# Pooled attention and a softplus FFN on one core: one transpose for a chunk's last keys, and new priorities for the first part

## The chip, the core and the metric

The kernel runs on one core of a Trainium2 chip. The metric is the device time in microseconds (us) of one execution; three executions of the kernel before took 883.39 to 884.7 us, with a median of 884.19. Five engines matter: TensorE (PE) for matrix products and transposes, VectorE (DVE), ScalarE (ACT), GpSimd (POOL, almost unused here) and SyncE (SP), which issues all the DMAs of the kernel in its own order.

## What is computed

Eight batches, eight heads, 576 tokens, 64 values per head. Keys and values are pooled by means over 8 tokens, so 72 of each remain per head. The attention output of all heads, 512 values per token and 4608 tokens, goes through a feed-forward network of width 2048 with a softplus between.

```python
k_p = k.reshape(B, H, Sp, pool, D).mean(axis=3)          # Sp = 72, pool = 8
v_p = v.reshape(B, H, Sp, pool, D).mean(axis=3)
scores = scale * np.matmul(q, k_p.transpose(0, 1, 3, 2))
scores = scores - np.max(scores, axis=-1, keepdims=True)
attn = np.exp(scores)
attn = attn / (np.sum(attn, axis=-1, keepdims=True) + 1e-09)
x = np.matmul(attn, v_p)              # -> (4608, 512): heads side by side
h = x @ w_in                          # w_in 512 x 2048
g = np.maximum(h, 0.0) + np.log1p(np.exp(-np.abs(h)))
out = g @ w_out                       # w_out 2048 x 512
```

All inputs are float32. For the large products each operand is split into a rounded high part and the rest (the low part), and three products stand for one.

## The kernel before

Tokens are taken in chunks of 256, two tiles of 128 each; there are 18 chunks. A chunk goes through attention (transposes of queries, scores, exponentials, normalisation, transposes of the probabilities, products with the values) and then through the FFN in 16 blocks of 128 hidden values.

The program has two parts, each planned by itself. The first, which ends near 182 us, loads and pools the first batches, converts the weights (seven DVE and ACT steps per block, in `weights`), runs attention for chunks 0 to 3 and the FFN for chunks 0 to 2. The second part runs the rest at a steady pace.

The order inside a part is made by a planner in the kernel's Python code, the class `Order`. Each operation has an engine, a cost in us, the operations it comes after, slots (buffers and PSUM banks that it takes and frees) and a lag. The planner goes forward in its own time: it finds the operation that could end first, and among those that the same engine could start about then it takes the one with the highest `rank + first`. `rank` is the length of the longest chain behind the operation; `first` is a correction. A table named `HASTE` adds such corrections by the operation's number:

```python
for i, x in HASTE.items():
    todo.ops[i + 2].first += x
```

So HASTE and the costs set the order of the first part on PE, ACT, DVE and SP, and which slot each operation gets; they add no instruction. For SP the costs are those of issuing, and the lag of 2.2 or 2.4 us stands for the time until the data has landed. An engine runs its instructions in the planned order and waits on the chip until the real inputs are there.

A query tile of `attend(c)`, chunk c, has 72 probabilities per head: 64 "main" ones and 8 "last" ones. `main` (L447) multiplies the 64 by the reciprocal sum into `pm`, `PT` (L468) transposes them and `PT_out` (L475) copies them. For the last 8 the kernel before does this, tile by tile: `ends` (L454, two DVE instructions) writes the products into `pe` three times side by side, 96 columns for each half of the heads; `last` (L480, two matmuls) transposes them into 96 rows of a PSUM bank; `last_high` (L487, one ACT cast) rounds all 96 rows into the tile `lt_`; `last_low` (L492, one DVE subtraction) turns the middle 32 rows into the low part. `av_products` (L594, L601) needs `pT` and `lt_` of both tiles.

The second part already does it by chunk: `pair_ends` (L563), `pair_last` (L568), `pair_high` (L574) and `pair_low_ends` (L578), for both tiles together.

Exponentials of chunks 0 to 2 are single ACT instructions per head with a running sum (`exp_sum`, L432); those of chunk 3 are one instruction. Exponentials and softplus (L632) use different ACT tables, and every softplus of the first part waits for all exponentials of chunks 0 to 2 (`*exps` in `feed`). The first load of softplus' table is recorded at L632.

Other lines: L347 warm-up products, L358 loads of queries, L387 and L394 transposes and copies of queries, L407 scores, L414 row minima, L906 and L909 loads of weights, L938 to L969 their conversion, L1002 and L1013 loads of keys and values, L1026 the products of the left-over tokens, L1060 and L1067 pooling of keys, L1084 pooling of values, L611 the low part of x, L627 and L652 the two FFN products of the first part, L638 the low part of g.

Of the kernel before, what the change touches and what calls it, by code (L numbers as in the profile page):

```python
# [9 lines left out]
F32 = mybir.dt.float32  # L10
# [98 lines left out]
def pooled_attention_softplus_ffn(  # L109
# [269 lines left out]
    class Tile:  # L379
# [47 lines left out]
        def exp_sum(self, j, ps, tag):  # L427
            if j == 0:
                self.sm = small.tile([P, H], F32, tag="sm" + tag, name="sm")
# [20 lines left out]
        def ends(self):  # L450
            self.pe = one.tile([P, 2, 3, R], F32, tag="pe", name="pe")
            for a in range(2):
                hs = slice(4 * a, 4 * a + 4)
                nc.vector.tensor_tensor(  # L454
                    out=self.pe[:, a].rearrange("p n (h j) -> p n h j", h=4),
                    in0=e_[self.c][:, self.t, hs, KM:SP].unsqueeze(1).to_broadcast([P, 3, 4, KL]),
                    in1=self.sm[:, hs].unsqueeze(1).unsqueeze(3).to_broadcast([P, 3, 4, KL]),
                    op=ALU.mult)

        def norm(self):  # L460
            self.reciprocal()
            self.main()
            self.ends()

# [12 lines left out]

        def last(self, ps):
            for a in range(2):
                nc.tensor.transpose(out=ps[0:3 * R, a * P:(a + 1) * P],  # L480
                                    in_=self.pe[:, a].rearrange("p n k -> p (n k)"), identity=ident)

        def last_high(self, ps):

            if self.c not in last_:
                last_[self.c] = one.tile([3 * R, 2, CT], F32R, tag="Y", name="lt_")
            nc.scalar.copy(out=last_[self.c][:, :, self.ts],  # L487
                           in_=ps[0:3 * R, 0:2 * P].rearrange("p (a i) -> p a i", a=2))

        def last_low(self, ps):  # L490
            o = last_[self.c][R:2 * R, :, self.ts]
            nc.vector.tensor_tensor(  # L492
                out=o, in0=ps[R:2 * R, 0:2 * P].rearrange("p (a i) -> p a i", a=2),
                in1=o.bitcast(F32), op=ALU.subtract)
# [384 lines left out]
    def act(n):  # L879
        return 0.14 + 0.00094 * n  # L880
# [10 lines left out]
    def weights(f):  # L891
# [5 lines left out]
        def load(i):  # L897
            def fn():
                if early:
                    if not i:  # L900
                        x["raw"] = stage_at(f % NS)
# [11 lines left out]
            return op(SYNC, 1.5, fn, slots=[stages[0 if early else i]], lag=2.2)  # L913
# [74 lines left out]
        op(SYNC, 0.9, lambda: nc.sync.dma_start(  # L988
# [585 lines left out]
```

## Time and profile before

| what | value |
|---|---|
| runs, median (lowest to highest) | 884.19 us (883.39 to 884.7) |
| the profiled execution | 883.75 us, span 882.0 us |
| PE busy, share of the span | 867.7 us, 98% |
| DVE, ACT busy | 645.4 us (73%), 418.3 us (47%) |
| mean granted clock of PE | 0.998 |
| DMA | 191.17 MB, mean 217 GB/s |

The span goes from the first to the last instruction; the profiled execution took 1.75 us more. An engine is busy while one of its instructions runs. "Idle" is told with the thing that ended it, which is inferred from semaphores. Where a name is followed by `x2`, two instructions are merged into one row.

### The profile page before, as it was taken

How to read it: one execution, taken by the hardware profiler on the slowest of the kernel's cores; microseconds unless marked ns; L12 is line 12 of the kernel's file. 1: busy time of each engine (PE TensorE's matmuls, PEld its weight loads, DVE VectorE, ACT ScalarE, POOL GpSimd, SP SyncE). 2: the span in 40 equal slices, each digit the busy share in tenths (PEclk: the TensorE clock that was granted, in tenths of full speed). 3: DMA queues.
4: the chain of work that ended last, by engine and by line, in shares of the span. 5: the costliest groups of instructions: out<-in, count | busy, mean ns of one | idle time of the engine just before them, and what ended most of it. 6: DMA issues, size and time to landing. Idle time of an engine off the chain costs nothing.

```text
span 882.0 us, 21268 instructions
## 1 busy us (share of the span) xinstructions
PE 867.7 (98%) x8664; PEld 843.3 (96%) x8664; DVE 645.4 (73%) x1601; ACT 418.3 (47%) x852; POOL 3.8 (0%) x33
## 2 busy tenths in 40 slices
PE   6999999999999999999999999999999999999997
PEld 3699999999999999999999999999999999999997
DVE  5899999888966868687767766778566565747454
ACT  5964443445454544544444445353545354444432
POOL 1000000000000000000000000000000000000000
PEclk9999999999999999999999999999999999999999
DMA  9975545545888668578757775778566566646472
GB/s 270 286 233 184 196 150 169 173 161 174 290 268 268 219 216 283 196 267 249 244 191 256 241 240 192 229 240 260 192 201 228 181 214 207 215 165 224 166 249 82
DMA packets 107089, 191.17 MB, mean 217 GB/s; under 512 B 46064, under 2 KB 60400, under 8 KB 106992
## 3 DMA queue, kind: packets, MB, share of 16 engines
q1 hardware_dynamic: 106992, 189.82, 64.4%
q8 instruction: 68, 1.11, 0.5%
q14 instruction: 29, 0.24, 0.1%
HBM read 167.25 MB, written 22.54 MB: 215 GB/s over the span
## 4 chain that ended last, share of the span: by engine, by line
PE 92%; DVE 3%; SPq 2%; DMA 2%; ACT 1%; issue 0%; DVEq 0%; ACTq 0%
PE h L680 38%; PE m L832 30%; PE acc L652 6%; PE h L627 6%; PE acc L723 3%; PE avp L594 2%; PE sc L515 1%; PE ptp L468 1%; PE qTp L387 1%; PE avp L601 1%; DMA stage<-in_moe_w_out_dram 1%; DMA kvl<-in_v_dram 1%; SPq L358 1%; DMA lst<-in_v_dram 1%; SPq L1013 0%
## 5 line engine op out<-in xcount | busy, mean ns | idle before, releaser
L680 PE MATMUL h<-x,l 128*128 128x256 f32 x2748 | 335.0, 278 | 0.0
L680 PEld LDWEIGHTS h<-x,l 128*128 128x128 f32 x2748 | 321.0, 188 | 1.0
L688 ACT ACTIVATE g<-h 128x512 f32<-128x512 f32 x120 | 71.9, 599 | 263.6 <-PE h L680 263.4
L832 PE MATMUL m<-w,so 128*128 128x256 f32 x1134 | 147.1, 276 | 0.0
L832 PEld LDWEIGHTS m<-w,so 128*128 128x128 f32 x1134 | 137.1, 188 | 0.1
L742 DVE TENSOR_TENSOR sf<-g 128x128 f32<-128x128 f32 x112 | 32.7, 292 | 134.2 <-ACT g L688 134.2
L756 ACT CAST so<-sf 128x512 fp32r<-128x512 f32 x112 | 69.7, 622 | 69.1 <-DVE sf L745 68.3
L832 PE MATMUL m<-w,gh 128*128 128x256 f32 x476 | 91.2, 280 | 0.0
L761 DVE TENSOR_TENSOR so<-sf,so 128x512 fp32r<-128x512 f32 x112 | 77.3, 690 | 18.2 <-ACT so L756 16.5
L832 PEld LDWEIGHTS m<-w,gh 128*128 128x128 f32 x476 | 71.7, 188 | 0.0
L709 DVE TENSOR_TENSOR gl<-g,gh 128x384 fp32r<-128x384 f32 (+1 forms) x120 | 67.4, 561 | 2.8 <-ACT gh L702 2.8
L832 PE MATMUL m<-w,gl 128*128 128x256 f32 x238 | 65.8, 277 | 0.0
L702 ACT ACTIVATE gh<-h 128x384 fp32r<-128x384 f32 (+1 forms) x120 | 59.1, 493 | 0.0
L632 ACT ACTIVATE g<-h 128x256 fp32r<-128x256 f32 x96 | 32.0, 382 | 54.3 <-PE h L627 32.4
L627 PE MATMUL h<-x,w 128*128 128x256 f32 x396 | 49.8, 278 | 0.2 <-ACT g L632 0.2
L627 PEld LDWEIGHTS h<-x,w 128*128 128x128 f32 x396 | 47.1, 188 | 0.6 <-ACT g L632 0.4
L652 PE MATMUL acc<-w,g 128*128 128x256 f32 x264 | 47.0, 279 | 0.0
L832 PEld LDWEIGHTS m<-w,gl 128*128 128x128 f32 x238 | 44.7, 188 | 0.0
L853 DVE TENSOR_TENSOR o<-o,m 128x256 f32<-128x256 f32 x98 | 39.8, 419 | 3.3 <-ACT o L845 0.4
L652 PEld LDWEIGHTS acc<-w,g 128*128 128x128 f32 x264 | 39.8, 188 | 0.1
L652 PE MATMUL acc<-w,gl 128*128 128x256 f32 x132 | 36.6, 277 | 0.5 <-DVE gl L638 0.5
L832 PE MATMUL m<-l,gh 128*128 128x256 f32 x196 | 37.0, 277 | 0.0
(210 smaller groups left out, 1318.2 us busy)
## 6 DMA issues: line engine op xcount, KB each, us to landing
l<-wi SPq DMA_DIRECT2D x224, 512.0 KB
out_dram<-o SPq DMA_DIRECT2D x36, 256.0 KB
q<-in_q_dram SPq DMA_DIRECT2D x32, 256.0 KB
kst<-in_k_dram SPq DMA_DIRECT2D x24, 288.0 KB
vst<-in_v_dram SPq DMA_DIRECT2D x24, 256.0 KB
stage<-in_moe_w_in_dram SPq DMA_DIRECT2D x22, 256.0 KB
stage<-in_moe_w_out_dram SPq DMA_DIRECT2D x11, 512.0 KB
wi<-w SPq DMA_DIRECT2D x11, 512.0 KB
```

The lines of the kernel that those rows point to most:

```text
L627: nc.tensor.matmul(out=ps[:, 0:CT], lhsT=row(w, kc), rhs=x[:, kc], start=first and kc == j == 0, stop=last and kc == KC - 1 and j == 2)
L632: nc.scalar.activation(out=g, in_=ps[:, 0:CT], func=AF.Softplus)
L652: nc.tensor.matmul(out=accs[c][t][:, ns], lhsT=a[:, ts], rhs=w[:, ns], start=f == 0 and n == j == 0, stop=f == FC - 1 and n == 1 and j == ...
L680: nc.tensor.matmul(out=ps[:, k * CT:(k + 1) * CT], lhsT=row(w, kc), rhs=x_[c][i][:, kc], start=first and n == 0, stop=last and n == len(or ...
L688: nc.scalar.activation(out=g, in_=x.rearrange("p (b i) -> p b i", i=P), func=AF.Softplus)
L702: nc.scalar.activation(out=gh, in_=quarters(c, x.rearrange("p (b i) -> p b i", i=P)), func=AF.Softplus)
L709: nc.vector.tensor_tensor(out=gl, in0=quarters(c, g), in1=gh.bitcast(F32), op=ALU.subtract)
L742: tt(out=sf[:, 2], in0=g[:, 0], in1=g[:, 2], op=ALU.add)
L756: nc.scalar.copy(out=so[:, 0], in_=ss[c, u])
L761: nc.vector.tensor_tensor(out=so[:, 1], in0=sf, in1=so[:, 0].bitcast(F32), op=ALU.subtract)
L832: nc.tensor.matmul(out=ms[c][n], lhsT=x, rhs=y, start=u == 0 and j == 0 and n in (1, 6, 5, 4), stop=u == FP - 1 and j == 2 and n in (2, 7, ...
L853: nc.vector.tensor_tensor(out=o, in0=in0, in1=m[n], op=how)
```

## The change

- In the first part too, the last keys are now handled by chunk, with the functions of the second part. `ends`, `norm`, `last`, `last_high` and `last_low` are removed. Per tile there is one `pair_ends` instruction; per chunk there are one pair of transposes, four casts of 32 rows and two subtractions.
- The slot `pe` belongs to a chunk, not to a tile.
- The order in which parts of a thing are first touched is free: `exp_sum` makes its sum tile at the first call, whichever half of the heads it is, and a weight block takes its staging tile at the first of its two loads.
- Costs in the planner are set anew (loads of weights 1.5 to 1.65, of keys and values 1.5 to 1.85, of queries 1.4 to 1.0, stores of converted weights 0.9 to 1.3, FFN products 1.4 to 1.37, the first products on PE higher).
- HASTE is replaced by a table with many more entries. As the change is described, the order of the first 31 loads was held while it was made.
- A way to take all exponentials of a chunk at once is added and switched off (`AT_ONCE = ()`).

```diff
@@ class Tile
         def exp_sum(self, j, ps, tag):
-            if j == 0:
+            if not hasattr(self, "sm"):
                 self.sm = small.tile([P, H], F32, tag="sm" + tag, name="sm")
...
-        def ends(self):
-            self.pe = one.tile([P, 2, 3, R], F32, tag="pe", name="pe")
...
-        def norm(self):
-            self.reciprocal()
-            self.main()
-            self.ends()
...
-        def last(self, ps):
...
-        def last_high(self, ps):
...
-        def last_low(self, ps):
...
@@ weights(f)
-                    if not i:
+                    if "raw" not in x:
...
-            return op(SYNC, 1.5, fn, slots=[stages[0 if early else i]], lag=2.2)
+            return op(SYNC, 1.65, fn, slots=[stages[0 if early else i]], lag=2.2)
...
-        op(SYNC, 0.9, lambda: nc.sync.dma_start(
+        op(SYNC, 1.3, lambda: nc.sync.dma_start(
@@ batch(b)
-        o_left = op(SYNC, 1.3, load_left, slots=[ld], lag=2.2)
-        o_k = [op(SYNC, 1.5, load(k, i), slots=[st[i]], lag=2.2) for i in range(2)]
-        o_v = [op(SYNC, 1.5, load(v, i), slots=[vt[i] or vt[0]], lag=2.2) for i in range(2)]
+        o_left = op(SYNC, 1.35, load_left, slots=[ld], lag=2.2)
+        o_k = [op(SYNC, 1.85, load(k, i), slots=[st[i]], lag=2.2) for i in range(2)]
+        o_v = [op(SYNC, 1.85, load(v, i), slots=[vt[i] or vt[0]], lag=2.2) for i in range(2)]
...
-        o = op(PE, 1.0, left_products, [o_left], [ld, s_left])
+        o = op(PE, 1.0 if b else 1.4, left_products, [o_left], [ld, s_left])
...
-            halves.append(op(PE, 0.1 + 0.28 * N, products, [o, *halves], [st[i], s_k]))
+            halves.append(op(PE, 0.1 + 0.28 * N + (0.4 if b == 0 and i else 0), products, ...
...
-        o = op(PE, 0.45, lambda: k_transposes(bank(s_t, "kT"), x["kp"]), [o, o_kl], [s_kp, s_t])
+        o = op(PE, 0.45 if b else 0.7, lambda: k_transposes(bank(s_t, "kT"), x["kp"]), [o, o_kl],
+               [s_kp, s_t])
@@ attend(c)
-            o_q.append(op(SYNC, 1.4, load,
+            o_q.append(op(SYNC, 1.0, load,
...
-        norms = []
+        norms, s_pe = [], Slot("pe")
...
-            o = op(PE, 0.5, lambda x=x, s=s_q: x.qT(bank(s, "qTp")),
+            o = op(PE, 0.5 if c else (1.1, 0.75)[t], lambda x=x, s=s_q: x.qT(bank(s, "qTp")),
...
-            o = op(DVE, 1.45, x.norm, ends, [*s_E, s_sm, s_pm, s_pe])
+
+            def norm(x=x):
+                x.reciprocal()
+                x.main()
+                pair_ends(c, x, "")
+            o = op(DVE, 1.27, norm, ends, [*s_E, s_sm, s_pm, s_pe])
             e_c.append(o)
-            s, r = Slot("bank"), Slot("bank")
+            s = Slot("bank")
             p = op(PE, 0.5, lambda x=x, s=s: x.PT(bank(s, "ptp")), [o], [s, s_pm])
             lows.append(op(ACT, act(512), lambda x=x, s=s: x.PT_out(s.tile), [p], [s, s_pT]))
-            p = op(PE, 0.3, lambda x=x, r=r: x.last(bank(r, "ltp")), [o], [r, s_pe])
-            h = op(ACT, act(256), lambda x=x, r=r: x.last_high(r.tile), [p], [r, s_lt])
-            lows.append(op(DVE, dve2(256), lambda x=x, r=r: x.last_low(r.tile), [h], [r, s_lt]))
+        s_l = Slot("bank")
+        p = op(PE, 0.25, lambda: pair_last(c, bank(s_l, "ltp")), e_c, [s_l, s_pe])
+        for a in range(2):
+            h = op(ACT, act(256), lambda a=a: pair_high(c, a, s_l.tile, a), [p], [s_l, s_lt])
+            lows.append(op(DVE, dve2(256), lambda a=a: pair_low_ends(c, a, s_l.tile), [h], [s_l, s_lt]))
+        for a in range(2):
+            lows.append(op(ACT, act(256), lambda a=a: pair_high(c, a, s_l.tile, 2), [p], [s_l, s_lt]))
@@ feed(c)
-            before1 = op(PE, 1.4, lambda f=f, s=s: ffn1_products(c, f, bank(s, "h")),
+            before1 = op(PE, 1.37, lambda f=f, s=s: ffn1_products(c, f, bank(s, "h")),
...
-                before2 = op(PE, 1.4, second, [before2, d], [gh, gl, *acc_slots[c]],
+                before2 = op(PE, 1.37, second, [before2, d], [gh, gl, *acc_slots[c]],
...
-    HASTE = {27: -130, 29: -3, 34: -120, 36: -120, 45: 40, 46: 20, 48: -180, 55: -2, 56: -10,
...
+    HASTE = {-2: -1844, -1: 13.6, 0: 1314.2, 1: 1554.7, 2: 1533.4, 3: 346.4, 4: 83.2, 5: 55.3, 6:
...
```

The functions that the first part now calls stood in the kernel already, for the second part:

```python
def pair_ends(c, x, tag):
    if c not in pe_:
        pe_[c] = one.tile([P, T, H, KL], F32, tag="pe", name="pe")
    nc.vector.tensor_tensor(out=pe_[c][:, x.t], in0=e_[c][:, x.t, :, KM:SP],
                            in1=x.sm.unsqueeze(2).to_broadcast([P, H, KL]), op=ALU.mult)

def pair_last(c, ps):
    for t in range(T):
        nc.tensor.transpose(out=ps[0:2 * R, t * P:(t + 1) * P],
                            in_=pe_[c][:, t].rearrange("p h k -> p (h k)"), identity=ident)

def pair_high(c, a, ps, row):
    if c not in last_:
        last_[c] = one.tile([3 * R, 2, CT], F32R, tag="Y", name="lt_")
    nc.scalar.copy(out=last_[c][row * R:(row + 1) * R, a], in_=ps[a * R:(a + 1) * R, 0:CT])

def pair_low_ends(c, a, ps):
    rows, to = (slice(i * R, (i + 1) * R) for i in (a, 1 - a))
    nc.vector.tensor_tensor(out=last_[c][to, a], in0=ps[rows, 0:CT],
                            in1=last_[c][rows, a].bitcast(F32), op=ALU.subtract)
```

More of the change, by code (lines that the diff above doesn't have):

```diff
@@ L476, in PT_out @@
                            in_=ps.rearrange("p (m i) -> p m i", m=HP))
-        def last(self, ps):
-            for a in range(2):
-                nc.tensor.transpose(out=ps[0:3 * R, a * P:(a + 1) * P],
-                                    in_=self.pe[:, a].rearrange("p n k -> p (n k)"), identity=ident)
-        def last_high(self, ps):
[L485 to L488, printed above, removed]
-        def last_low(self, ps):
[L491 to L494, printed above, removed]
     order_dep = mybir.DependencyInfo(mybir.DependencyClass.Sync, mybir.DependencyReason.DATA)
@@ L1068, in products @@
                                      rhs=x["k", i][:, :, r], start=r == 0, stop=r == N - 1)
-            halves.append(op(PE, 0.1 + 0.28 * N, products, [o, *halves], [st[i], s_k]))
+            halves.append(op(PE, 0.1 + 0.28 * N + (0.4 if b == 0 and i else 0), products, [o, *halves], [st[i], s_k]))
         o = op(ACT, act(512), lambda: nc.scalar.copy(
@@ L1094, in pooled_attention_softplus_ffn @@
     qT_done, score_done, av_done, k_ready, v_ready, made = {}, {}, {}, {}, {}, {}
+    AT_ONCE = ()
     def attend(c):
@@ L1130, in attend @@
                        [s, s_mn])
-                if c < N1:
+                if c < N1 and c not in AT_ONCE:
                     def exp_sum(x=x, i=i, s=s, e=s_E[0], t=t, n=s_sm):
-                        if c == 0 and 0 not in e_:
+                        if 0 not in e_:
                             new_E(0)
@@ L1140, in less @@
                     def less(x=x, i=i, s=s):
-                        if c not in e_:
+                        if c in AT_ONCE:
+                            if 0 not in e_:
+                                new_E(0)
+                            e_[c] = e_[0]
+                        elif c not in e_:
                             new_E(c)
                         x.less(i, s.tile)
-                    ends.append(op(DVE, 0.46, less, [d, *e_free], [s, s_mn]))
-            if c < N1:
+                    ends.append(op(DVE, 0.46, less, [d, *(e_free if c == N1 else ())], [s, s_mn, *s_E]))
+            if c in AT_ONCE:
+                o = op(ACT, 0.68, lambda x=x: exponential(e_[c][:, x.t]), ends, s_E, table="exp")
+                exps.append(o)
+                ends = [op(DVE, 0.76, lambda x=x, n=s_sm: x.sum(n.name), [o], [s_sm, *s_E])]
+            elif c < N1:
                 exps.extend(ends)
```

13 lines of the change are left out of this document (3 added, 10 removed), and 92 rows, old and new, of the table HASTE.

## The prediction

> **What bounds the kernel now.** I read the page first, then a table of stages, then TensorE's waits in the early stage, and last the rows of the instructions that the change touches.
>
> ```profile
> span 882.0 us, 21268 instructions
> PE 867.7 (98%) x8664; PEld 843.3 (96%) x8664; DVE 645.4 (73%) x1601; ACT 418.3 (47%) x852; POOL 3.8 (0%) x33
> ```
>
> TensorE (PE) is busy 867.7 of 882.0 us, so no order of the work can take out more than 14.3 us, and less work on PE shortens the kernel only where PE is full. The table of stages says where that is (columns: the stretch and its length, then busy time and instructions of PE, PE weight loads, DVE, ACT and POOL, granted clock, DMA share, GB/s):
>
> ```profile
> 0.00:20.00 20.00, 13.23 (x106) 6.95 (x106) 12.05 (x22) 10.17 (x41) 2.36 (x19) 0.91 0.91 261
> 20.00:46.00 26.00, 23.36 (x308) 17.62 (x307) 21.24 (x51) 23.76 (x93) 0.00 (x0) 1.00 0.96 299
> 46.00:182.00 136.00, 135.69 (x1264) 133.74 (x1264) 126.35 (x228) 59.39 (x135) 0.00 (x0) 1.00 0.54 177
> 182.00:870.00 688.00, 688.00 (x6932) 677.89 (x6931) 480.39 (x1290) 322.95 (x582) 1.46 (x14) 1.00 0.66 223
> 870.00:882.00 12.00, 7.40 (x64) 7.10 (x62) 5.36 (x14) 1.98 (x4) 0.00 (x0) 1.00 0.11 44
> ```
>
> The first part of the program ends near 182 us. PE stands idle 6.77 us before 20, 2.64 from 20 to 46, 0.31 from there to 182, never from 182 to 870, and 4.60 in the drain at the end, which the change does not touch. So whatever the first part saves on PE moves the end by as much, and all that a new order can save lies before 46 us. The waits of PE in 0 to 45 us (who waited, for whom, total, times, longest):
>
> ```profile
> PE qTp L387 <- DVE stage L943: 2.3, 1, 2.3
> PE warm L347 <- DVE ones L342: 1.5, 1, 1.5
> PE kps L1067 <- DVE kvst L1060: 1.1, 1, 1.1
> PE kvlp L1026 <- DMA kvl<-in_v_dram: 1.0, 1, 1.0
> PE kps L1067 <- DMA kvst<-in_k_dram: 0.8, 1, 0.8
> PE ltp L480 <- DVE pe L454: 0.8, 2, 0.5
> PE avp L594 <- DVE lt__503 L492: 0.4, 1, 0.4
> PE sc L407 <- ACT qT L394: 0.3, 1, 0.3
> PE ptp L468 <- DVE x L611: 0.2, 1, 0.2
> PE sc L407 <- ACT kT L265: 0.2, 1, 0.2
> ```
>
> The first five rows, 6.7 us, are the start of the program and arriving data. The 2.3 us are put down to a DVE instruction that has nothing to do with queries; a transpose of queries waits for its load, so I read that row as a DMA. The last five, 1.9 us, are matters of order between engines. Two of them, 1.2 us together, hang on the very tiles that the change reworks, pe and lt.
>
> The early stage has a second loss, the clock:
>
> ```profile
> 12.20:15.80 3.60, 0.63 (x4) 0.95 1.11 295
> 15.80:19.20 3.40, 3.36 (x9) 0.55 0.98 274
> L1067 PE MATMUL kps<-kvst,zm x20: 379/390/660, 6.0 to 27.6; 128*64 128x256 f32 x20
> ```
>
> Behind 3.6 us in which PE (first figure after the length) worked 0.63, the granted clock fell to 0.55 for the next 3.4 us; the key products there took up to 660 ns where the shortest took 379. At full clock this stretch is worth about 3.4 x (1 - 0.55) = 1.5 us less.
>
> **The change part by part.**
>
> *Transposes on PE.* Each tile now has a transpose of its pe, as a pair of matmuls; afterwards each chunk of two tiles has one pair. Eight pairs become four. What a pair costs is read from its start to the next start, once in the loose early stage and once in the dense one:
>
> ```profile
> 25.22 0.42 PE L480 MATMUL ltp<-ident,pe 128*96 128x128 f32 x2
> 25.48 0.60 PE L468 MATMUL ptp<-ident,pm 128*128 128x128 f32 x4
> 71.07 0.38 PE L480 MATMUL ltp<-ident,pe 128*96 128x128 f32 x2
> 71.21 0.96 PE L627 MATMUL h<-x,w 128*128 128x256 f32 x6
> ```
>
> 0.26 us early, 0.14 late. Three pairs go from the stretch before 50 us and one from the dense stretch: 3 x 0.26 + 0.14 = 0.92 us at most, and 0.14 at least, if the early ones only lengthen waits. I take -0.5.
>
> *The products pe on DVE.* Per tile two instructions of 96 columns become one of 64:
>
> ```profile
> L563 DVE TENSOR_TENSOR pe<-E,sm x28: 216/219/223, 212.8 to 816.6; 128x64 f32<-128x64 f32 x28
> L454 DVE TENSOR_TENSOR pe<-E,sm x16: 250/252/254, 18.7 to 68.2; 128x96 f32<-128x96 f32 x16
> ```
>
> The new form is already run in the second part of the program (first row). 8 x (2 x 0.252 - 0.219) = 2.3 us of DVE time go. DVE is 82% busy in 20 to 46 and 93% after, and PE hardly waits for it after 46, so I price this at nothing by itself; it shortens the two waits of PE on pe and lt, which are in the holes below.
>
> *The casts on ACT.* This is the part that costs. Per chunk two casts of 96 rows become four of 32 rows, and rows cost no time:
>
> ```profile
> L487 ACT CAST lt__372<-ltp x2: 369/370/371, 22.6 to 25.7; 96x256 fp32r<-96x256 f32 x2
> 218.93 0.74 ACT L574 CAST lt__3134<-ltp 32x256 fp32r<-32x256 f32 x2 [0.77 <-PE ltp L568]
> 219.70 0.41 DVE L578 TENSOR_TENSOR lt__3134<-ltp,lt__3134 32x256 fp32r<-32x256 f32 x1 [1.33 <-ACT lt__3134 L574]
> 220.15 0.36 ACT L574 CAST lt__3134<-ltp 32x256 fp32r<-32x256 f32 x1 [0.48 <-DVE lt__3134 L578]
> 220.54 0.41 DVE L578 TENSOR_TENSOR lt__3134<-ltp,lt__3134 32x256 fp32r<-32x256 f32 x1 [0.42 <-ACT lt__3134 L574]
> 220.99 0.36 ACT L574 CAST lt__3134<-ltp 32x256 fp32r<-32x256 f32 x1 [0.48 <-DVE lt__3134 L578]
> 41.95 1.28 ACT L632 ACT_TABLE_LOAD   x1
> ```
>
> Eight more casts of 0.36 us, 2.9 us in all, six of them for the three early chunks: 2.2 us. And the second part shows how they run: cast, low part and cast on one tile wait for each other in turn, 218.93 to 221.35, 2.4 us, and ACT, which works in order, stood 0.48 us twice. Behind such a cast wait the exponentials of the next tile, and behind the last exponential the table load at 41.95 and every softplus; PE waits for that. From 20 to 46 ACT is busy 23.76 of 26 us, so 2.24 us of slack. Lower end 0 (the casts fill ACT's gaps, or stand behind the table load), upper end 2.2 + 3 x 2 x 0.48 = 5.1 less 2.24 of slack = +2.9. I take +0.5, nearer the lower end, since only the casts of two chunks need come before the table load.
>
> *Slot of pe.* It is held for a chunk now, not a tile, so the next chunk's products wait for this chunk's one transpose. The two norms of a chunk follow each other on DVE anyway: nothing, up to 0.3 where a transpose is late.
>
> *Priorities and the planner's costs.* No instruction and no DMA is added or dropped by them; they set the order of PE, ACT, DVE and SP up to 182 us. With the order of the first loads held, the five waits for start and data (6.7 us) mostly stay. In reach are the 2.64 us of 20 to 46 and 0.31 behind, 2.95 in all: from 0 to -2.95, and below that a loss if new waits come up. I take -1.8: the 1.2 us on pe and lt have half their instructions gone, and a third of the other 1.75. For the start I take -0.4 of the 6.7 + 1.5 us. This end is open on both sides: SP has one wait that an order could shorten,
>
> ```profile
> SPq L358 <- PE qTp L387: 4.5, 2, 2.7
> ```
>
> a load of queries held up to 2.7 us until a transpose on PE had read the buffer. If that transpose goes sooner, the load does; if it goes later, every load queued on SP behind it is late too.
>
> *Second part.* Its plan begins from the first one's ends, but PE is busy 688.00 of 688.00 us there: nothing.
>
> *Sum.* -0.5 + 0.5 - 1.8 - 0.4 = -2.2 us. The profiled execution took 883.75 us, 1.75 more than its span, which gives 881.55. The median of the runs, 884.19, lies 0.44 above that execution, so the time I predict on the runs' scale is 884.19 - 2.2 = **882.0 us**. A measurement of this kernel can tell about 0.2%, 1.77 us, from no change: faster means below 882.4, slower above 886.0.
>
> **The rivals.**
>
> *The holes at the start close too* (chance 0.16). The 2.7 us wait of SP speaks for it: transposes of the first queries put ahead of other early PE work let the load go sooner. Then about half of the 2.3 us hole goes, 1.0, and the slow clock behind it, 1.45: -2.2 - 2.45 = -4.65, 879.5 us. Against it: held loads, with a DMA share of 0.91 already before 20.
>
> *The holes move, they do not close* (0.22): the priorities do not do what they are set for. The planner counts 2.2 us from issue to landing, whatever the load of the DMA engines, which are 0.96 busy from 20 to 46; an order that is tight by its own costs meets late data elsewhere. Then -0.5 and +0.5 stay and a quarter of the holes, -0.7: 883.5 us.
>
> *The clock* (0.08): PE is thinned out again ahead of a dense stretch and a second stretch of 3.4 us runs at 0.55: +1.5 on the forecast, -0.7, 883.5 us. The Trainium skill, in "TensorE: Matmul & The Clock Gate", Part 1: The HAM clock gate, says that the slow clock is the default, that about one window of 3.4 us without enough work brings it back, and that the windows run freely; the trace agrees with that (0.63 us of work in 3.6, then 0.55). By the rule the loss comes or goes whole, with the place of the work in the window; my sum holds a mean between.
>
> *ACT becomes the early bound* (0.20, slower). Place: ACT from 20 us to the table load. Price: all six casts and their six stalls ahead of it, 5.1 - 2.24 = +2.9 us, less 0.5 on PE: +2.4, 886.6 us. It decides from the point where casts and stalls together exceed 2.24 us. For it speaks the serial chain at 218.93; against it that the casts can wait behind the table load, as the row of 41.95 allows for the third chunk.
>
> **How the numbers follow.** The forecast has 0.34, with its own range of 880.7 to 882.4. Faster: 0.34 + 0.16 = 0.50. Within 0.2%: 0.22 + 0.08 = 0.30. Slower: 0.20. The range of 879.0 to 886.2 reaches from below the first rival to half of the last one.
>
> **What would show it.** After the change ltp must be eight matmuls with 64 columns up to 100 us, and pe eight instructions near 0.22 us. PE's idle time from 20 to 182 should fall from 2.95 to about 1.2, the first table load should stand near 41 us, and the span should be near 880. Right steps with a wrong total would show in PE's busy time: more than 1 us less of it would mean that the clock or the transposes were undersized. I am wrong if the table load comes later than 43 us, if ACT waits for low parts before it, if SP issues one of the early loads later than now, or if PE has new waits between 46 and 150, where DVE has little to spare.

## The result, and the profile after

The kernel after takes 889.5 us (median of 6 runs, 886.42 to 890.55), the kernel before beside it 884.39 us (6 runs, 882.84 to 884.92). The ratio is 1.0057 with a 95% interval of 1.004 to 1.0074: slower by about 5 us, where 2.2 us less had been forecast. Three executions of the kernels below, of 969 to 2233 us, were disturbed and stand in no median here.

The profiled execution took 889.96 us. Its page begins so:

```profile
span 888.2 us, 21256 instructions
PE 870.5 (98%) x8656; PEld 846.0 (95%) x8656; DVE 645.0 (73%) x1593; ACT 420.5 (47%) x860; POOL 3.8 (0%) x33
```

The span is 6.2 us longer than the 882.0 of before. PE has 8 matmuls less, and is busy 2.8 us *more*; it also stands idle 3.4 us more. Both need an explanation. The table of stages, with the columns of the prediction's table:

```profile
0.00:20.00 20.00, 14.24 (x138) 7.54 (x138) 10.73 (x17) 8.72 (x30) 2.37 (x19) 1.00 0.88 255
20.00:46.00 26.00, 20.41 (x264) 14.90 (x254) 20.48 (x42) 21.19 (x91) 0.00 (x0) 0.98 0.96 295
46.00:182.00 136.00, 134.32 (x1208) 132.94 (x1209) 120.57 (x218) 59.73 (x143) 0.00 (x0) 0.99 0.50 164
182.00:870.00 688.00, 688.00 (x6946) 677.38 (x6945) 484.86 (x1298) 326.65 (x593) 1.47 (x14) 1.00 0.67 225
```

From 182 us on nothing has changed: PE is full. Idle time of PE is 5.76 us up to 20 (before 6.77), 5.59 from 20 to 46 (before 2.64) and 1.68 from 46 to 182 (before 0.31). The holes of 20 to 182, which the new order was to close, went from 2.95 to 7.27 us.

**Where the new idle time comes from.** PE's waits up to 46 us (who waited, for whom, total, times, longest):

```profile
PE avp L568 <- ACT lt__586 L541: 2.1, 1, 2.1
PE kps L1034 <- DVE kvst L1027: 1.6, 2, 1.1
...
PE avp L568 <- ACT lt__407 L541: 1.0, 1, 1.0
...
PE ltp L535 <- DVE pe L530: 0.3, 1, 0.3
```

Two of them, 3.1 us, hang on the casts into `lt_` (L541; names of lines are those of the kernel after). All engines' waits from 20 to 62 us name the chain behind them:

```profile
DVE stage L905 <- DMA stage<-in_moe_w_out_dram: 3.6, 2, 2.4
ACT lt__586 L541 <- DVE lt__586 L545: 2.9, 1, 2.9
...
ACT lt__407 L541 <- DVE lt__407 L545: 1.8, 1, 1.8
```

And the timeline shows it in order of time (start, length, instruction, and in brackets how long its engine was idle before and what ended that):

```profile
33.70 0.47 SPq L873 DMA_DIRECT2D stage<-in_moe_w_out_dram  x1
...
41.80 0.69 DVE L905 TENSOR_SCALAR stage<-stage 128x1024 int32<-128x1024 int32 x1 [2.44 <-DMA stage<-in_moe_w_out_dram]
42.52 0.69 DVE L910 TENSOR_SCALAR stage<-stage 128x1024 f32<-128x1024 f32 x1
43.23 0.84 DVE L545 TENSOR_TENSOR lt__586<-ltp,lt__586 32x256 fp32r<-32x256 f32 x2
...
44.11 0.36 ACT L541 CAST lt__586<-ltp 32x256 fp32r<-32x256 f32 x1 [2.87 <-DVE lt__586 L545]
...
44.52 0.98 PE L568 MATMUL avp<-lt__586,vlo 96*128 96x256 f32 x4 [2.13 <-ACT lt__586 L541]
...
48.47 1.28 ACT L599 ACT_TABLE_LOAD   x1
```

A weight load issued at 33.70 has landed only by 41.8, 8.1 us later. DVE stands still for it with the first step of the weight's conversion. Behind that step in DVE's order are two low parts of chunk 1's last keys. Behind these the fourth cast waits on ACT: it writes other rows of `lt_` than the low parts and only reads, as the second of them does too, the same 32 rows of the transposes; it waits for them all the same. PE's products with the values wait for the cast, and behind the cast on ACT come exponentials, so the table load comes at 48.47, not 41.95. The same chain had run once before, for chunk 0, from 30.78 to 32.36 us. In the kernel before, the low parts of chunk 0 stood ahead of that conversion (rows of the kernel before, same view):

```profile
26.16 0.42 DVE L492 TENSOR_TENSOR lt__372<-ltp,lt__372 32x256 fp32r<-32x256 f32 x1
...
30.35 0.74 PE L601 MATMUL avp<-lt__372,vlo 96*128 96x256 f32 x4
30.89 0.69 DVE L938 TENSOR_SCALAR stage<-stage 128x1024 int32<-128x1024 int32 x1 [0.77 <-DMA stage<-in_moe_w_out_dram]
```

The load itself is nearly as late in the kernel before: that of the same block was issued at 33.19 us and landed at 39.16. There DVE comes to this block's first step only at 47.5 us, long after the low parts of chunk 1.

How much hangs on this chain differs between executions. after_flip (see The pace) has the same order up to 70 us; there the load had landed by 39.5 us, and PE waited 0.7 us for the casts in place of 3.1. Its idle time from 20 to 182 us was 6.36 us all the same. Two other waits stand in the profiled execution of every kernel with the new order, and not in those of before and before_again (rows of after_flip, then of order_alone, which has the old form of the last keys):

```profile
PE ptp L456 <- DVE pm L449: 1.7, 1, 1.7
...
PE sc L409 <- ACT qT L396: 1.3, 2, 1.0
...
PE avp L571 <- ACT lt__586 L544: 0.4, 1, 0.4
```

```profile
PE ptp L463 <- DVE pm L447: 2.4, 2, 1.9
```

In the first, the transposes of chunk 2's second tile stand in PE's order ahead of FFN products, while ACT still computes that tile's exponentials (1.3 us near 50 us in after, 1.7 to 1.9 in the six others). In the second, scores near 21 us wait 0.97 us for the copy of their queries, in before 0.29. Neither hangs on the casts.

**Where the longer busy time comes from.** The table of stages over a stretch in which PE is full in both kernels and runs almost only the FFN's 256-column products, first before, then after:

```profile
100.00:150.00 50.00, 50.00 (x444) 50.00 (x443) 47.46 (x86) 20.17 (x49) 0.00 (x0) 1.00 0.51 173
```

```profile
100.00:150.00 50.00, 50.00 (x427) 50.00 (x426) 43.91 (x73) 18.79 (x46) 0.00 (x0) 1.00 0.39 131
```

In the same 50 us at the same granted clock of 1.00, PE did 444 products before and 427 after: 112.6 against 117.1 ns each. The groups of the first FFN product from 60 to 170 us (count: shortest/median/longest ns) tell the two apart too, before and after:

```profile
L627 PE MATMUL h<-x,w x335: 276/276/386, 59.8 to 148.7; 128*128 128x256 f32 x168
```

```profile
L594 PE MATMUL h<-x,w x348: 276/281/385, 61.9 to 147.7; 128*128 128x256 f32 x174
```

So the same product has two paces: a recorded length of 276 ns goes with 113.3 ns from start to start (mean of the gaps between neighbours from 100 to 150 us), 281 ns with 117.8. A pace holds for a whole dense stretch and changes at the small groups between (four transposes, scores). After the change one unbroken stretch of 744 products, 82.7 to 170.3 us, ran at the slow pace: 744 x 4.5 ns = 3.3 us. The kernel before had a shorter slow stretch, 1.5 us, between 185 and 250 us, which the kernel after has not (0.4).

The sum for the two profiled spans, in us: idle time from 20 to 182 +4.3, and pace up to 250 us +2.1 (the gaps between neighbouring products above 113.3 ns, added up: 4.4 against 2.25). In the opening the clock became full only at about 10.7 us, where before it was full from 5.2 on (rows below); half of PE's busy time until then makes +2.1, and PE, working slower, waited 1.0 less for the loads. Each has one more stretch at half the clock, of 3.4 us, and the difference there is 0.2. That makes +7.7; the spans differ by 6.2, so some 1.5 us of PE's work are gone. The opening's share is chance: before_again, the same program as before, was at full clock only from 10.6 us on. Without it (+2.1 and -1.0) the difference is 5.1 us, about that of the medians.

### The profile page after: what moved, and what is told of

The parts are those of the page before. It is cut to its first block, busy times and chain, and to the rows that moved or that the text cites. A ratio compares the mean times of both kernels' runs of the same rounds, so it can differ in the third digit from the quotient of the medians.

```text
span 888.2 us, 21256 instructions
## 1 busy us (share of the span) xinstructions
PE 870.5 (98%) x8656; PEld 846.0 (95%) x8656; DVE 645.0 (73%) x1593; ACT 420.5 (47%) x860; POOL 3.8 (0%) x33
## 4 chain that ended last, share of the span: by engine, by line
PE 94%; DMA 3%; DVE 2%; SPq 1%; ACT 0%; issue 0%; DVEq 0%; ACTq 0%
PE h L647 37%; PE m L799 30%; PE acc L619 7%; PE h L594 7%; PE acc L690 2%; PE avp L561 2%; PE qTp L387 2%; PE ptp L453 2%; PE sc L482 1%; PE avp L568 1%; DMA kvst<-in_k_dram 1%; DMA stage<-in_moe_w_out_dram 1%; DMA vst<-in_v_dram 1%; PE kps L1034 1%; PE ltp L535 0%; PE m L482 0%
## 5 line engine op out<-in xcount | busy, mean ns | idle before, releaser
L594 PE MATMUL h<-x,w 128*128 128x256 f32 x396 | 52.0, 286 | 0.3 <-DVE x L578 0.2
L594 PEld LDWEIGHTS h<-x,w 128*128 128x128 f32 x396 | 49.2, 193 | 0.9 <-DVE x L578 0.4
```

Of the source, the lines that this page charges most:

```text
L594: nc.tensor.matmul(out=ps[:, 0:CT], lhsT=row(w, kc), rhs=x[:, kc], start=first and kc == j == 0, stop=last and kc == KC - 1 and j == 2)
```

## The experiments

Each is compared with the kernel before in runs beside it. The table collects them: ratio of times with its interval; PE's idle time up to 20 us and from 20 to 870 us; the loss to the clock (half of PE's busy time while the granted clock was half, or ahead of the first record of the clock); the loss to the pace up to 250 us, as above; what is then left over of the span's difference from before, which is work added or taken out and the error of this reckoning; the recorded length of the FFN's products in 60 to 170 us; the profiled span. All but the ratio and ns in us. One profiled execution stands for each kernel, while the times spread over some 3 to 6 us.

| kernel | ratio (95%) | idle to 20 | idle 20 to 870 | clock | pace | left over | ns | span |
|---|---|---|---|---|---|---|---|---|
| before | 1 | 6.77 | 2.95 | 3.2 | 2.2 | 0 | 276 | 882.0 |
| after | 1.0057 (1.004 to 1.0074) | 5.76 | 7.27 | 5.5 | 4.4 | -1.5 | 281 | 888.2 |
| pair_alone | 1.0077 (1.0047 to 1.0106) | 5.95 | 3.65 | 7.8 | 5.9 | -1.0 | 281 | 889.3 |
| order_alone | 1.0088 (1.0065 to 1.0112) | 5.43 | 8.52 | 6.6 | 2.6 | 0.4 | 276 | 890.4 |
| casts_first | 1.004 (1.0025 to 1.0056) | 4.04 | 6.51 | 6.5 | 1.3 | -1.4 | 276 | 883.9 |
| lows_first | 1.0055 (1.0032 to 1.0078) | 6.13 | 7.61 | 3.3 | 1.0 | -1.0 | 276 | 883.9 |
| both | 1.007 (1.0049 to 1.009) | 3.97 | 7.53 | 6.7 | 1.4 | -1.2 | 276 | 885.2 |
| before_again | 0.999 (0.9975 to 1.0006) | 6.41 | 2.45 | 5.5 | 0.7 | -0.4 | 276 | 881.5 |
| before_flip | 1.0035 (1.0016 to 1.0055) | 6.29 | 2.40 | 7.6 | 4.5 | 0.4 | 281 | 888.0 |
| after_flip | 1.0052 (1.0034 to 1.0071) | 5.76 | 6.36 | 5.6 | 4.3 | -0.6 | 281 | 888.4 |
| pair_012 | 0.9997 (0.9984 to 1.001) | 5.84 | 2.60 | 8.5 | 1.2 | -1.8 | 276 | 883.3 |
| before_warm | 0.9987 (0.9975 to 1.0) | 4.65 | 2.18 | 3.9 | 0.6 | 2.5 | 276 | 880.7 |
| after_warm | 1.0068 (1.0055 to 1.0081) | 3.89 | 6.62 | 4.3 | 4.5 | 0.9 | 281 | 887.2 |
| pair_012_warm | 1.0008 (0.9997 to 1.002) | 5.18 | 2.85 | 1.9 | 1.4 | 2.4 | 276 | 880.7 |

The seven kernels with the new order are idle 6.4 to 8.5 us from 20 us on, the seven with that of before 2.2 to 3.7. That part of the loss belongs to the order. Clock and pace fall differently within either group.

### Half of the change at a time

*The pairing in the order of before* (pair_alone): costs, HASTE and order of before, the last keys by chunk, their four casts and two low parts at the second tile's places.

```diff
             self.main()
-            self.ends()
+            pair_ends(self.c, self, "")
...
+            def high(x=x, r=r):
+                if x.t == 1:
+                    for a in range(2):
+                        pair_high(c, a, r.tile, a)
+                    for a in range(2):
+                        pair_high(c, a, r.tile, 2)
```

> The kernel before with its own costs and priorities; only the last keys are handled by chunk: both tiles' products pe stay where they were, and the one pair of transposes, the four casts and the two low parts stand where the second tile's stood. Theory A (late data in front of the low parts, and the serial use of the tile lt, both made by the new order): the pairing by itself costs next to nothing, 883 to 885.5 us, the first softplus table load between 41.5 and 43 us, no wait of a matmul on lt above 1 us. Theory B (the added casts fill ACT, as the prediction's slower rival has it): the table load comes 2 to 3 us later and the time is 886 to 887 us.

*The new order with the old form* (order_alone): HASTE, costs and order of after, but `ends`, `last`, `last_high` and `last_low` per tile, at the places of the chunk's operations.

```diff
-                pair_ends(c, x, "")
+                x.ends()
...
-            h = op(ACT, act(256), lambda a=a: pair_high(c, a, s_l.tile, a), [p], [s_l, s_lt])
+            h = op(ACT, act(256), high, [p], [s_l, s_lt])
```

> The changed kernel's order on every engine, but the last keys tile by tile in the old form (three copies of pe, two pairs of transposes, one cast of 96 rows and one low part per tile), each put at the place of the new form's instructions. Theory A: DVE still stands in front of weights that have not landed, so the low parts come as late as before and the value products wait about 2 us for lt near 42 to 44 us; but both casts stand ahead of the low parts, so ACT does not stand 2.9 us and the table load comes near 45 to 46 us instead of 48.5: 886 to 888 us. Theory B: without the added casts the new order brings what it was made for, 881 to 883 us. If the new order itself is bad throughout: 889 to 890 us.

Measured: 890.74 us and 890.93 us, where before has 882.97. Either half alone is as slow as the whole change, and for different reasons; no expectation has either time. In pair_alone idle time from 20 us on is near that of before (3.65 against 2.95), but see its stages, PE's one wait of over 0.2 us in 60 to 100 us, and the rows around it:

```profile
60.00:100.00 40.00, 38.98 (x331) 38.51 (x330) 37.13 (x58) 19.26 (x40) 0.00 (x0) 1.00 0.59 194
100.00:150.00 50.00, 50.00 (x427) 50.00 (x426) 45.99 (x80) 19.14 (x46) 0.00 (x0) 1.00 0.47 160
```

```profile
68.78 1.48 ACT L574 CAST lt__1010<-ltp 32x256 fp32r<-32x256 f32 x4 [1.01 <-PE ltp L568]
...
70.28 0.66 ACT L632 ACTIVATE g<-h 128x256 fp32r<-128x256 f32 x2
...
71.00 1.65 PE L627 MATMUL h<-x,w 128*128 128x256 f32 x12 [0.86 <-ACT g L632]
```

Chunk 3's four casts, 1.48 us in a row, stand ahead of a softplus in the dense stretch; PE waits 0.86 us for it, and from 72.8 to 173 us runs at the slow pace, 427 products in 50 us. In order_alone the pace is the fast one, and PE is idle 4.30 us from 20 to 46, 2.81 from there to 182 and 1.24 from 182 to 200:

```profile
20.00:46.00 26.00, 21.70 (x295) 16.34 (x296) 21.89 (x48) 21.61 (x95) 0.00 (x0) 1.00 0.98 302
46.00:182.00 136.00, 133.19 (x1217) 131.46 (x1216) 121.61 (x224) 58.89 (x140) 0.00 (x0) 0.99 0.50 165
182.00:200.00 18.00, 16.76 (x149) 15.92 (x148) 14.13 (x28) 8.37 (x19) 0.00 (x0) 1.00 0.49 187
```

So the idle time belongs to the new order, not to the form of the last keys. For order_alone the idle time (-1.3 up to 20 us, +5.6 from there on), the clock (+3.4) and the pace (+0.3) make 8.0 of the 8.4 us by which its span is longer.

### The chain of the late weights

*The fourth cast ahead of the low parts* (casts_first), for chunks 0 and 1: the same instructions as after, two of them moved in the emitted order. *The conversion behind the low parts* (lows_first): the first DVE steps of weight blocks 1 and 2 moved behind the low parts of chunks 0 and 1. *Both* moves together (both).

```diff
-        for o in todo.run():
+        order = todo.run()
+        for n, where, other in [(264, 'after', 260), (298, 'after', 296)]:
+            o = next(x for x in order if x.i == n)
+            order.remove(o)
...
+        for o in order:
             o.fn()
```

lows_first has this list in its place, and both has the two lists together:

```diff
+        for n, where, other in [(54, 'after', 261), (64, 'after', 295), (65, 'after', 64)]:
```

> The changed kernel with two casts moved: the last cast of chunks 0 and 1 goes directly behind the other casts of its chunk, ahead of the low part on which it waits now. Nothing else moves. Theory A: the waits of ACT on DVE's low parts (1.8 and 2.9 us) vanish, the last exponentials and the table load come 2.5 to 3 us sooner (45.5 to 46 us), while the value products still wait for the low part itself, so that only part of the loss returns: 886 to 888 us. If ACT's stall does not matter because PE waits for the low part anyway: 889 to 890 us.

> The changed kernel with DVE's order changed at two places: the first conversion step of weight block 1 goes behind the low part that it precedes, and the first two steps of block 2 go behind both low parts of chunk 1. ACT, PE and SP keep their order. Theory A: DVE no longer stands in front of late weights while a low part waits behind it, so the value products of chunk 1 start near 41.5 us without a wait, ACT does not stand, the table load comes near 45 us, the clock stays at 1.0, and 3 to 5 us return: 884 to 886 us. If the late weights are only a symptom (the conversions that slip then bring new waits of PE before 60 us): 887 to 889 us.

> The changed kernel with both repairs of the early stage: the last casts of chunks 0 and 1 ahead of the low parts, and DVE's conversion steps that stood in front of late weights behind the low parts. Each alone brought 2 to 3 us in the medians. Theory A (the two are one chain: late weights hold the low part, the low part holds the cast, the cast holds the exponentials): together hardly more than the better one alone, 885.5 to 887 us. If they are two losses that add up: 883 to 885 us.

Measured: 886.75, 887.87 and 889.4 us. With the fourth cast ahead, ACT does the four of chunk 1 in one go, while DVE still converts (casts_first, timeline):

```profile
39.85 1.47 ACT L541 CAST lt__586<-ltp 32x256 fp32r<-32x256 f32 x4
39.88 0.68 DVE L905 TENSOR_SCALAR stage<-stage 128x1024 int32<-128x1024 int32 x1
...
41.35 0.84 DVE L545 TENSOR_TENSOR lt__586<-ltp,lt__586 32x256 fp32r<-32x256 f32 x2
...
43.28 0.74 PE L568 MATMUL avp<-lt__586,vlo 96*128 96x256 f32 x4
```

The products with the values come at 43.28, not 44.52, and the table load at 46.37, not 48.47. But the load had landed at 39.48 here, against 41.67 in after, so part of this is the data's. In after_flip, where the casts stand as in after and the load landed at 39.52, these products come at 42.37 and the table load at 46.31. Idle time from 20 us on is 6.51 us, between after_flip and after. So the trace of after shows the chain at work once; that moving the cast helps (ratio 1.004 against 1.0057) is not shown, as the intervals overlap. The other two moves don't help: in lows_first and in both the late conversion holds up PE elsewhere (PE waits 1.1 us for w, L936), and idle time is 7.61 and 7.53. The 2 to 3 us in the expectation of both come from medians of two separate sets of runs; by the ratios to before beside them, the two moves are worth 1.5 and 0.2 us.

lows_first settles another point. Its profiled execution has *more* idle time than after, up to 20 us and behind, and a span of 883.9, 4.3 us shorter. Its clock took 2.2 us less, and it ran the long stretch at the other pace, worth 3.4 us:

```profile
L594 PE MATMUL h<-x,w x348: 276/276/385, 60.2 to 143.8; 128*128 128x256 f32 x174
```

### The pace

*Before once more* (before_again): nothing changed. *Before with a perturbation* (before_flip): the four transposes of chunk 3's second pm, ahead of the long stretch, are done twice, 0.43 us more work. *After with the same* (after_flip).

```diff
-            for n in range(HP):
+            again.append(self.c)
+            for n in [*range(HP)] * (2 if again.count(N1) == 2 and self.c == N1 else 1):
```

> The kernel before, unchanged, profiled a second time. In the traces so far two things differ that no instruction of the program explains: whether the first products after the warm-up run at full clock (a key product at 6 us takes 0.62 us for two in the first trace of this kernel, 1.08 in others), and the pace of back-to-back matmuls in the long stretch from about 72 to 167 us (median 276 ns in the first trace, 281 in those of the changed kernel and of the pairing alone). Theory C (the changed kernel loses most of its time to the pace of matmuls, which its order sets): here the long stretch shows 276 ns again, whatever the opening does, and the time is 881 to 885 us. If the pace is mere chance from run to run: 281 ns may show up here, with a time above 886 us.

> The kernel before with one thing added: the four transposes of chunk 3's second tile of probabilities, which stand shortly ahead of the long stretch of FFN products, are done twice into the same bank (0.43 us more of PE). Theory C, with what the traces show so far (four such transposes between dense products change the pace, eight leave it as it was): the long stretch runs at a median of 281 ns, some 840 matmuls cost 4.5 ns more each, and the time rises by 0.4 + 3.8 us to about 887 us. If the pace has nothing to do with it: 0.4 us more, 883 to 884 us.

> The changed kernel with the same addition: the four transposes of chunk 3's second tile are done twice. Theory C: the long stretch, 744 matmuls at 281 ns in the changed kernel's trace, now runs at 276 ns, which gives back 3.3 us for 0.4 us spent: 886 to 887 us in most runs. If the loss sits in the early waits alone: 889.5 to 890.5 us.

Measured: 883.55, 886.97 and 887.78 us, before beside them 884.02. Four transposes more make before 3.4 us slower than before_again, where their own work is 0.43 us; the long stretch ran at the slow pace in the profiled execution:

```profile
L630 PE MATMUL h<-x,w x348: 276/281/388, 60.8 to 154.5; 128*128 128x256 f32 x174
```

A change of the work that is worth 0.05% moved the time by 0.35%. The rule behind the expectation does not hold, though. In before_flip the products ahead of the eight transposes are fast and those behind them slow. In before_again, with four transposes, they are fast ahead and fast behind; in before, with four as well, slow ahead and fast behind. In after_flip the same edit did not bring the fast pace: the stretches ahead of it began otherwise than in after, and the long one ran at 281 ns again. Which group flips the pace to which side can't be told in advance from these runs. The program alone does not fix it: from 182 to 215 us before ran at the slow pace and before_again, the same program, at the fast one (1.45 against 0.35 us lost from 185 to 250).

### Chunk 3 in the old form, and a warm opening

*The pairing for chunks 0 to 2 only* (pair_012): as pair_alone, but chunk 3, whose last keys fall in the dense stretch, keeps `ends`, `last`, `last_high` and `last_low`.

```diff
             self.main()
-            self.ends()
+            if self.c == N1:
+                self.ends()
+            else:
+                pair_ends(self.c, self, "")
```

> The pairing in the order of before, for chunks 0 to 2; chunk 3, whose last keys fall in the dense stretch, keeps the old form. Theory: pairing alone was slow since the four casts of chunk 3 stood ahead of a softplus near 70 us (PE stood still 0.86 us at 71) and the long stretch ran at 281 ns a matmul. Expected then: no wait of PE between 60 and 100 above 0.2 us, 276 ns in the long stretch, 883 to 885 us, ratio 0.9985 to 1.0015. Rival: the pairing is slow by its casts in 20 to 46 us: the ratio stays at 1.005 or above, with PE idle from 20 to 46 above the 2.6 us of before by 2 us or more. Third possibility: the idle time goes as the theory says, but the pace is 281 ns all the same: 886 to 888 us.

Measured: 883.28 us (before 883.83). The stages of pair_012, and its FFN products:

```profile
60.00:100.00 40.00, 39.85 (x349) 39.55 (x349) 38.80 (x62) 18.90 (x40) 0.00 (x0) 1.00 0.60 198
100.00:150.00 50.00, 50.00 (x444) 50.00 (x443) 47.72 (x85) 20.16 (x48) 0.00 (x0) 1.00 0.50 164
```

```profile
L630 PE MATMUL h<-x,w x348: 276/276/383, 60.5 to 150.9; 128*128 128x256 f32 x174
```

The whole loss of pair_alone, some 7 us by the ratios, is gone when chunk 3 keeps the old form. Of the 6.1 us between the two profiled spans, 0.86 are the wait and 4.7 the pace of the stretch behind it (5.9 against 1.2). That chunk 3's pairing always brings the slow pace is not shown; the change itself has its pair elsewhere, near 183 us. The pairing of the three early chunks costs nothing in the time; that it gains cannot be told either (0.9984 to 1.001). It makes a wait of its own, scores near 36 us behind ACT's four casts in a row,

```profile
PE sc L407 <- ACT pT L478: 1.2, 1, 1.2
```

and the 1.2 us that PE waited for pe and lt in before are gone. The first table load came at 44.39 us in pair_012, 44.65 in pair_alone and 44.47 in before_flip, which has no pairing, against 41.95 in before: some 2.5 us later, and here without a price.

*The longer warm-up* in before, after and pair_012 (before_warm, after_warm, pair_012_warm): 256 columns more at the start, and nine unused 128-column products in PE's first gaps.

```diff
-    op(PE, 3.6, lambda: warm(x_w[0], bank(s_w, "warm"), (512, 384)), [o], [s_w], first=2000)
+    op(PE, 3.6, lambda: warm(x_w[0], bank(s_w, "warm"), (512, 384, 256)), [o], [s_w], first=2000)
...
+            if b == 0:
+                warm(ident, ps, (128,) * 3)
...
+            if len(asked) == 3:
+                warm(ident, ps, (128,) * 6)
```

The reason are the first key products in the profiled executions of before, of before_again, of after and of pair_012. The work is the same:

```profile
5.95 0.62 PE L1067 MATMUL kps<-kvst,zm 128*64 128x256 f32 x2 [1.08 <-DVE kvst L1060]
```

```profile
5.92 1.08 PE L1067 MATMUL kps<-kvst,zm 128*64 128x256 f32 x2 [1.05 <-DVE kvst L1060]
```

```profile
5.95 1.08 PE L1034 MATMUL kps<-kvst,zm 128*64 128x256 f32 x2 [1.08 <-DVE kvst L1027]
```

```profile
5.95 1.08 PE L1070 MATMUL kps<-kvst,zm 128*64 128x256 f32 x2 [1.08 <-DVE kvst L1063]
```

> Theory (opening clock): the warm-up of the kernel before ends at 4.9 us and PE then stands idle and thin, so that in many executions the full clock is granted only at 10 to 17 us, and the early matmuls take about double: 1.5 to 4 us of PE time lost. Edit: the warm-up is 256 columns longer, three unused 128-column matmuls stand ahead of the first kvlp, and six ahead of the third transposes of queries, all in gaps of PE. Expected: key products near 6 us at 0.62 us a pair, not 1.08; no slow stretch up to 20 us; span about 1.5 to 2.5 us shorter, 881.5 to 882.5 us on the scale where the kernel before has 884, ratio 0.997 to 0.9985. Rival (data): the opening is bound by loads that arrive late, and a faster PE only waits longer for them: ratio 0.9995 to 1.0005, the idle time up to 20 us larger by what the matmuls lose. Second rival: the fillers run at the slow clock and stand in the way of work: slower by 1 to 2 us, ratio 1.001 to 1.002.

> The same edit in the kernel after. If the opening clock makes up a part of the loss of the change, this kernel comes down by more than the kernel before does: from 1.0055 to about 1.001 to 1.002. If the change's loss lies in the order of 20 to 60 us and in the pace of the long stretch, as the idle time (+4.3 us) says, it comes down by as much as the kernel before or less, 0 to 2.5 us, and stays at 1.0025 or above.

> Both edits together: the pairing of chunks 0 to 2 in the order of before, and the longer warm-up with its fillers. If both theories hold, 0.5 us less work of PE for the pairing and 1.5 to 2.5 us from the clock: 881 to 882 us, ratio 0.9965 to 0.998, below both kernels. If pairing is slow in itself, above before_warm by 3 us or more; if the pace of the long stretch decides, this kernel lands at either of two places 3.5 us apart.

Measured: 882.33, 889.19 and 884.37 us (before 883.83). In before the edit is worth 1.1 us in the middle of the interval, which reaches to nothing, and it did not do all that was expected: a slow stretch still stands at 16.7 us. after_warm tells little: its fillers did not keep the clock up, the second six ran slow themselves (2.93 us, where the same take 1.60 in before_warm), and the time is that of after. That the slow opening is not what made the change slow is seen better in pair_012, whose opening was slow for longer (1.08 us in the row above, full clock at about 14 us) and whose span is 883.3. In before_warm PE, with 1.6 us of fillers just ahead, still waits 2.0 us for the third load of queries (a row of PE's waits):

```profile
PE qTp L392 <- DMA q<-in_q_dram: 2.0, 1, 2.0
```

Its transposes start at 15.61 us there, at 14.43 in before. So this place of the opening is bound by the load, as the rival in the expectation has it; how much of the rest is, these runs do not show. pair_012_warm is no sum of two gains. No kernel here beats before by more than can be measured.

## Why the prediction was wrong, step by step

*What bounds the kernel.* The table of stages was read rightly for idle time: from 182 us to the drain nothing moves. Its other half was wrong: "busy" was taken for work, so that only less work or less idle time could count. PE's busy time for the same products differs by 4% with the pace. This failed step has no term in the sum. The pace is worth 3.3 us in the long stretch, and 2.1 between the two spans.

*Transposes, -0.5.* Right as far as it can be seen: the matmuls of ltp have 64 columns as foretold, though chunk 3's pair comes only near 183 us, behind the long stretch. What is left of the spans after idle time, pace and clock is 1.5 us less work, where the upper bound was 0.92. The kernels with pairing and without fillers have 0.6 to 1.8 us less by this reckoning, those without pairing lie within 0.4 of before; so a saving is there, and its size is not told closer than to about half a microsecond.

*pe on DVE, nothing.* Right: eight instructions at the price of the second part (the row of the tile pe), and 0.3 us of PE's waits on them. The rows of the tile ltp up to 100 us, behind it, bear on transposes and casts.

```profile
L530 DVE TENSOR_TENSOR pe<-E,sm x8: 216/219/222, 21.7 to 79.8; 128x64 f32<-128x64 f32 x8
```

```profile
L535 PE MATMUL ltp<-ident,pe x6: 271/285/300, 24.9 to 53.5; 128*64 128x128 f32 x6
L541 ACT CAST lt__407<-ltp x4: 359/361/363, 26.2 to 31.9; 32x256 fp32r<-32x256 f32 x4
```

*Casts on ACT, +0.5, at most +2.9.* The 0.36 us of one are right. The place and kind of the loss are not. ACT was not short of time: it is busy 21.19 us from 20 to 46, less than the 23.76 of before. Casts in a row don't stall either (four in 1.47 us above). But the row that the prediction quoted, cast, low part and cast waiting for each other, was priced at 0.48 us a stall, the length of a low part and a hop; in the profiled execution of after the low part itself waited for late data, and the stalls were 2.87 and 1.77 us. What the term left out is that such a wait lasts as long as whatever stands ahead of the other side. And chunk 3's casts, counted as harmless "behind the table load", held up a softplus in the dense stretch where they came in one row (pair_alone): 0.86 us there.

*Slot of pe, 0 to 0.3.* At most the 0.3 us of PE's wait on pe, as bounded.

*Priorities, -1.8.* This is the step that failed most: the holes of 20 to 182 grew by 4.3 us. Its working does not give its number either: half of the 1.2 us on pe and lt and a third of 1.75 make 1.2, not 1.8, which takes the 1.2 in full. pair_012 shows that the pairing does take these waits away, in the order of before. But the term looked only at holes that were there, and took it that a new order would close a third of the others; nothing in the trace bore that out. In place of it new waits came up: for chunk 2's last probabilities (1.3 to 1.9 us) and for the copy of queries (0.97) in every kernel with the new order, and for the casts behind a late load (3.1 in after, 0.7 in after_flip), a load that takes 8.1 us where the planner counts 2.2. order_alone, with the old form of the last keys, is idle as long. Which entries of the new table make these waits was not tried.

*Start, -0.4.* Idle time up to 20 us fell by 1.0, and PE's slow clock until 10.7 us took 2.1 more: no gain. That the clock's phase differs between executions of one kernel was not in the sum.

*The rivals.* "The holes move, they do not close" had a mechanism that the trace of after shows, loads later than the planner counts, and a wrong size: it kept a gain of 0.7 us, where the holes grew by 4.3; and in other executions most of that growth is there without the load being so late. "ACT becomes the early bound" came nearest in time (886.6) and named the chain of cast and low part and the late table load, but as a matter of ACT's slack; that its time is near is luck. The clock rival happened in part: a slow stretch stands at another place,

```profile
44.80:48.30 3.50, 3.46 (x17) 3.17 (x17) 3.30 (x7) 3.50 (x19) 0.00 (x0) 0.51 1.07 398
```

behind PE's 2.13 us wait, about as costly as the one of before at 15.8 us, which is gone. after_flip and order_alone have one behind waits of 1.7 and 1.9 us, casts_first, with a wait of 1.7, has none. The signs named beforehand came true on the wrong side: the table load later than 43 us (48.47), ACT waiting for low parts ahead of it, the third load of queries issued at 11.17 us and not 10.78, and a new wait of PE near 50 us.

## What to carry to other kernels

An order that is tight by a planner's own landing times should be checked against the landing times in the trace: what stands behind a late load in an engine's order was late with it here, and so were the engines that waited for that work. One trace does not give the size: the same order lost 3.1 us to one load in one execution and 0.7 in another. Where the gain looked for is a few tenths of a per cent, first see how much the same kernel moves when a few instructions are added ahead of its dense stretch; here that was 3.4 us, more than the 2.2 that were forecast. Compare counts of like matmuls in equal stretches, not only busy shares.

## What the runs showed of the hardware

**Two paces of the same matmul.** 128 x 128 by 256 columns, back to back, at a granted clock of 1.00: 113.3 or 117.8 ns from start to start, 276 or 281 ns in the records. A stretch of several hundred keeps one of them. All five profiled executions with 281 ns in the long stretch have spans of 887.2 us and more, eight of the nine with 276 ns lie at 885.2 and less (the ninth is order_alone). The cause of the lock is not known from these runs.

**The opening's clock differs from execution to execution.** The same warm-up, 1.51 to 4.86 us, was followed by fast matmuls at 5.95 us in one execution of before and by slow ones until about 10.6 us in another (before_again). The Trainium skill says in "TensorE: Matmul & The Clock Gate", Part 1: The HAM clock gate, that the window of activity runs freely and does not begin with the kernel, so that the count of slow matmuls varies with its phase. The rows of before and before_again above agree with that: two key products took 0.62 us in the one and 1.08 in the other. The Trainium skill adds in the same place that a model should not be fitted to one such count.

**A wait beside other rows.** The fourth cast and the low parts write different rows of one tile, and read one bank of transposes; the cast waited up to 2.87 us for them. Whether the tile or the bank orders them, and whether that wait could be left out, was not tried; moving the cast was.
